# H and V of each octet in one block of TensorE, over three two-bank PSUM tiles

## The chip, the core and the metric

The kernel runs on one core of a Trainium2 chip. A core has a matrix engine (TensorE, PE in the profile, with its weight loads shown apart as PEld), a vector engine (VectorE, DVE), a scalar engine (ScalarE, ACT), GpSimd (POOL) and SyncE (SP), which here only issues transfers. Each engine works through its own list of instructions in order. The engines share SBUF, the working memory of 128 partitions, and PSUM, the memory that matmuls write, of 8 banks of 512 fp32 values per partition. DMA transfers are issued by SP, ACT or POOL and run beside the engines; a name with a q behind it (ACTq, SPq) is an engine's issuing part. The metric is the device time of one execution in microseconds (us).

## What is computed

Three terms are summed for a sequence of 2048 rows of 448 channels. Both branches take the layer-normalised first input.

```python
def _A_ref(q, k, v, shift_k, ssm_k, ssm_D):
    k_shift = sum of 4 shifted copies of k times shift_k       # short causal convolution
    kv = k_shift * v
    y = long causal convolution of kv with ssm_k, per channel (FFT of length 4096)
    return q * (y + kv * ssm_D)

def _B_ref(x, w1, b1, w2):
    h = einsum("bsd,df->bsf", x, w1) + b1                       # 448 -> 1792
    return einsum("bsf,fd->bsd", mish(h), w2)                   # 1792 -> 448

xn = _layernorm(A_q)
return A_q + _A_ref(xn, A_k, A_v, A_shift_k, A_ssm_k, A_ssm_D) + _B_ref(xn, B_w1, B_b1, B_w2)
```

## The kernel before

**The dense branch** is most of TensorE's work. It runs over 8 chunks of 256 rows and 7 pairs of 128-wide slices of the hidden layer, 56 pairs in all, numbered i. For each pair, `g1_mm(i)` makes the first product (22 matmuls of 256 columns, split into high and low parts XH, XL, w1h, w1l) in one PSUM bank; `mish(i)` reads that bank on ACT (two ACTIVATE), casts the result to `ach` on ACT and takes the rest `acl` on DVE; `g2_mm(i)` makes the second product (12 matmuls of 448 columns) in PSUM tiles `pg2`, two pairs later.

**Slots.** The program is written out by hand. Slot 2i holds `g1_mm(i)`. Slot 2i+1 holds `mish(i)` and `g2_mm(i-2)`. `at(slot, ...)` puts other work ahead of the dense work of a slot, `after(slot, ...)` behind it. No scheduler moves anything: the order written is the order on each engine. Small DVE pieces wait in a list `drip` and are taken out one by one by calls of `dv()`.

**The long convolution** goes through DRAM in stages. In slots up to 61 the columns of `ssm_k` and of `kv` are transformed (`f1_mm`) and stored to DRAM as Dh and Dkv. Then come 8 octets, the stage that is changed. For octet o:

- SP loads `ah` from Dh and `av` from Dkv (896 KB each) and the small factors `g` and `gi`.
- `h2_mm` makes H from `ah` in two PSUM tiles `pc` of two banks (real and imaginary part): 16 matmuls on 64x32 pieces of the array. `h2_out` copies H to SBUF (`hs`) on ACT, two copies.
- `v2_mm` does the same with `av` one slot later, and `v2_out` copies V to `vs` on ACT.
- `prod` multiplies both on DVE: six instructions of 128x896 (four products, one difference, one sum), in two parts in the two slots behind.
- `i1_mm` transforms the result back (16 matmuls on 32x64 pieces) into two `pc` tiles. `i1_out` copies them to `qe` on ACT, and ACT issues two stores to DRAM, to E.

V of octet o stands in slot 65+3o, H in the slot before it (octet 0: slot 63), the back transform in slot 69+3o, the last in slot 90. H, V and the back transform each stand ahead of the dense work of their slots, so each is a block of small matmuls between two runs of full-size ones. The tiles `pc` are taken in turn from a pool of two, four banks; the first product has two banks and the second two.

**The last transform.** From slot 92 POOL loads `e` from E (`e_load`), DVE folds each (`fold`, two instructions of 128x896), and `i2_mm` makes the last transform for two chunks at a time in slots 98, 102, 106 and 110, each followed by the gate with q. In the same slots the last chunk is normalised on DVE: `idr`, a row of means and factors, is loaded by SP (`nt_row`, slot 92 for its second half), `nt_norm` (two instructions, slot 94) uses it, and `nt_split` makes XH and XL of it. SP issues `q_load` for two chunks in slot 92, ahead of that row. The SBUF space of the octets is used again from slot 92 by tiles that wait until the last user of the space that they lie on is done.

## Time and profile before

| | us |
|---|---|
| median of 3 runs | 364.59 (364.45 to 365.19) |
| the profiled execution | 364.74 |
| its span, first to last instruction | 363.0 |
| PE busy | 357.0 (98% of the span) |
| DVE busy | 268.0 (74%) |
| ACT busy | 166.6 (46%) |
| POOL busy | 71.4 (20%) |

The profiled execution took 0.15 us more than the median. Around the span lie 1.74 us. An engine's busy time counts its instructions on the data; waiting and issuing are not in it. In rows of the timeline the first number is the start from the span's begin, the second the length, and `[... <-X]` is idle time before and what ended it. A row that ends in x16 stands for 16 records; TensorE shows two records for each fp32 matmul, so 16 matmuls of a block read x32. The granted TensorE clock was 1.00 in nearly all of the span.

### The profile page before, as it was taken

Reading aid. Unit: us, or ns where it says so; the run is one execution under the profiler, and the core shown is the slowest. Engines: PE = TensorE matmul, PEld = TensorE weight load, DVE = VectorE, ACT = ScalarE, POOL = GpSimd, SP = SyncE. Lnnn points to the kernel's source line nnn. Section 1 sums busy time; section 2 is a strip of 40 time slices with the busy share of each in tenths; the row PEclk is TensorE's granted clock in tenths of the full one; section 3 lists DMA queues with packets and bytes.
Section 4 is the critical chain, followed back from the end, with each engine's and each line's share of the span. In section 5 each row is a group of like instructions: output and inputs, shape, how many; then the busy total and the mean of one; then the engine's idle time right before and its main releaser. Section 6 shows DMA issues by size and latency. Waiting matters only on the chain.

```text
span 363.0 us, 7466 instructions
## 1 busy us (share of the span) xinstructions
PE 357.0 (98%) x3108; PEld 290.0 (80%) x3108; DVE 268.0 (74%) x367; ACT 166.6 (46%) x279; POOL 71.4 (20%) x66
## 2 busy tenths in 40 slices
PE   8999999999999999999999999999999999999995
PEld 2988888888888988988977666666666889889885
DVE  5999658999998988797427755767665744997641
ACT  4966553343424323334254555647655534225450
POOL 2136003722037224513000020000010005112020
PEclk9999999999999999999999999999999999999999
DMA  7998969758686438615877798998897486969655
GB/s 247 363 369 307 414 248 275 182 175 270 156 260 199 105 101 255 152 60 144 226 245 231 252 257 210 289 258 218 284 283 172 93 251 216 404 246 279 105 71 132
DMA packets 32451, 81.69 MB, mean 225 GB/s; under 512 B 2977, under 2 KB 18978, under 8 KB 32418
## 3 DMA queue, kind: packets, MB, share of 16 engines
q1 hardware_dynamic: 21266, 47.16, 39.3%
q10 hardware_dynamic: 8240, 19.38, 21.8%
q0 software_dynamic: 2912, 14.69, 13.5%
q8 instruction: 24, 0.39, 0.5%
q14 instruction: 9, 0.07, 0.1%
HBM read 52.77 MB, written 28.45 MB: 224 GB/s over the span
## 4 chain that ended last, share of the span: by engine, by line
PE 49%; DMA 4%; DVE 2%; ACT 1%; ACTq 1%; issue 0%
PE pg L499 18%; PE pg L528 7%; PE pc L219 6%; PE pg L530 6%; PE pg L529 6%; PE pc L262 4%; PE pc L319 2%; DMA av<-Dkv 2%; DMA Dkv<-st 2%; ACTq L273 1%; DVE st L140 1%; DVE x L183 1%; ACT a L507 0%; DVE qt L535 0%; DVE x L186 0%
## 5 line engine op out<-in xcount | busy, mean ns | idle before, releaser
L507 ACT ACTIVATE a<-pg,b1t 128x256 f32<-128x256 f32 x112 | 47.2, 473 | 108.7 <-PE pg L499 95.4
L499 PE MATMUL pg<-XH,w1h 128*128 128x256 f32 x448 | 90.6, 285 | 0.2 <-DVE XL L462 0.2
L499 PEld LDWEIGHTS pg<-XH,w1h 128*128 128x128 f32 x448 | 69.6, 188 | 18.6 <-issue 16.5
L528 PE MATMUL pg<-w2h,ach 128*128 128x448 f32 x224 | 83.2, 371 | 0.0
L530 PE MATMUL pg<-w2h,acl 128*128 128x448 f32 x224 | 81.4, 363 | 0.0
L80 DVE TENSOR_TENSOR acl<-a,ach 128x512 fp32r<-128x512 f32 x56 | 39.1, 698 | 57.1 <-ACT ach L79 57.0
L529 PE MATMUL pg<-w2l,ach 128*128 128x448 f32 x224 | 81.2, 362 | 0.0
L499 PE MATMUL pg<-XL,w1h 128*128 128x256 f32 x448 | 71.3, 277 | 0.0
L499 PEld LDWEIGHTS pg<-XL,w1h 128*128 128x128 f32 x448 | 60.2, 188 | 0.0
L499 PE MATMUL pg<-XH,w1l 128*128 128x256 f32 x336 | 56.8, 278 | 0.0
L528 PEld LDWEIGHTS pg<-w2h,ach 128*128 128x128 f32 x224 | 42.0, 187 | 14.4 <-issue 11.5
L499 PEld LDWEIGHTS pg<-XH,w1l 128*128 128x128 f32 x336 | 46.8, 188 | 0.0
L530 PEld LDWEIGHTS pg<-w2h,acl 128*128 128x128 f32 x224 | 42.1, 188 | 2.6
L529 PEld LDWEIGHTS pg<-w2l,ach 128*128 128x128 f32 x224 | 42.1, 188 | 2.4
L140 DVE TENSOR_TENSOR st<-pc,st 128x896 f32<-128x896 f32 x32 | 34.8, 1089 | 4.5 <-ACT st L136 3.8
L79 ACT CAST ach<-a 128x512 fp32r<-128x512 f32 x56 | 34.7, 620 | 1.8
L166 POOL TENSOR_TENSOR x<-kr,skb 128x896 f32<-128x896 f32 x8 | 17.0, 2130 | 78.2 <-DVE x L165 56.8
L183 DVE TENSOR_TENSOR x<-x 128x896 f32<-128x896 f32 x24 | 26.4, 1098 | 2.8 <-POOL x L166 2.2
L403 POOL TENSOR_TENSOR mv<-ve,mhalf 128x2 f32<-128x2 f32 x3 | 3.8, 1251 | 98.1 <-DVE ve L400 98.1
L136 ACT COPY st<-pc 128x896 f32<-128x896 f32 x16 | 14.5, 907 | 14.2 <-PE pc L130 12.6
L407 POOL TENSOR_SCALAR xn<-qt,mv,rstd 128x448 f32<-128x448 f32 x8 | 20.5, 2566 | 0.4
L270 ACT COPY qe<-pc 128x896 f32<-128x896 f32 x16 | 13.8, 912 | 12.0 <-PE pc L262 12.0
(83 smaller groups left out, 384.4 us busy)
## 6 DMA issues: line engine op xcount, KB each, us to landing
Dkv<-st ACTq DMA_DIRECT2D x16, 448.0 KB, 6.3
ah<-Dh SPq DMA_DIRECT2D x8, 896.0 KB, 7.9
av<-Dkv SPq DMA_DIRECT2D x8, 896.0 KB, 6.9
E<-qe ACTq DMA_DIRECT2D x16, 448.0 KB, 5.8
e<-E POOLq DMA_DIRECT2D x8, 896.0 KB, 8.4
kr<-in_k_dram SPq DMA_DIRECT2D x10, 448.0 KB, 6.4
Dh<-st ACTq DMA_DIRECT2D x10, 448.0 KB, 5.9
x<-in_hT_dram SPq DMA_DIRECT2D x8, 448.0 KB, 6.5
```

The costliest lines, as they stand in the source:

```text
L79: nc.scalar.copy(h, raw)
L80: V.tensor_sub(l, raw, h)
L140: f(st[:, n], e, st[:, 1])
L166: nc.gpsimd.tensor_mul(o, KR[g - u // 2], skb[:, u:u + 1].to_broadcast([128, 2, D]))
L183: V.tensor_add(KV[g], KV[g], o)
L219: nc.tensor.matmul(p[32 * t:32 * t + 32, r, :D], g[rs, t, c], a[rs, t], start=True, stop=True, tile_position=(64 * r, 32 * t))
L407: eng.tensor_scalar(xn[:, jj, :D], Q[c][:, jj], mv[:, j, 0:1], rs(c)[:, jj:jj + 1], op0=ALU.subtract, op1=ALU.mult)
L499: nc.tensor.matmul(ps[n], l, r, start=all(m[0] != n for m in seq[:n_]), stop=all(m[0] != n for m in seq[n_ + 1:]))
L507: nc.scalar.activation(a[:, n], ps[n], AF.Mish, bias=b1t[:, 2 * p + n:2 * p + n + 1])
L528: nc.tensor.matmul(ps, ah[:, n, cs], w2h[:, f], start=f == 0, stop=False)
L529: nc.tensor.matmul(ps, ah[:, n, cs], w2l[:, f], start=False, stop=False)
L530: nc.tensor.matmul(ps, al[:, n, cs], w2h[:, f], start=False, stop=f == NF - 1)
```

## The change

H and V of an octet become one block: `hv_mm(o)` issues the 16 matmuls of H, then the 16 of V, in slot 66+3o. The octets' back transform comes later: that of octet o-1 stands two slots behind octet o's block (the last two in slots 88 and 89).

V is no longer copied to SBUF. The four products on DVE read V straight from its PSUM tiles, so each V tile stays taken until two products have read it. `prod` is one piece behind the block: four products, then what is held back of `mish` in odd slots (its cast and `acl`), then difference and sum. In an odd slot with a block, `mish` is issued ahead of it.

PSUM: the two tiles `pq` and `pr` (two banks each) are made once for the whole program. `regroup(True)` in slot 66 closes the first product's pool of two banks and makes a third two-bank tile `pp` of them; `regroup(False)` in slot 92 turns it back. In between the first product writes a bank of whichever tile the table `GB` names. Each block therefore goes round: in an even slot H takes pp and pq, V takes pr and then pp again; in an odd slot H takes pr and pq, V takes pp and then pr again. So the second half of V waits until ACT has copied the first half of H.

SBUF: `av` gets a second buffer and is loaded a slot earlier; `hs` loses its second buffer, `vs` goes, `ya` and `yc` get a second one. The result of the last octet is copied to a buffer named `hs` instead of `qe`.

The stores to E are issued by GpSimd (`nc.gpsimd.dma_start`) instead of ACT.

On TensorE, an octet with its block in an odd slot stood so before, H and V on either side of a first product (`pc` the PSUM tiles, `pg` those of the dense branch):

```order
L219 MATMUL pc<-ah,g 32x448 x16
L499 MATMUL pg_2750<-XH,w1h 128x256 x3
L499 MATMUL pg_2750<-XH,w1l 128x256 x3
L499 MATMUL pg_2750<-XH,w1h 128x256
L499 MATMUL pg_2750<-XL,w1h 128x256 x4
L499 MATMUL pg_2750<-XH,w1h 128x256 x3
L499 MATMUL pg_2750<-XH,w1l 128x256 x3
L499 MATMUL pg_2750<-XH,w1h 128x256
L499 MATMUL pg_2750<-XL,w1h 128x256 x4
L219 MATMUL pc<-av,g 32x448 x16
```

Now an octet in an odd slot reads on TensorE, between the first product (which stands in pp) and the second:

```order
L508 MATMUL pp<-XH,w1h 128x256
L508 MATMUL pp<-XL,w1h 128x256 x4
L231 MATMUL pr<-ah,g 32x448 x8
L231 MATMUL pq<-ah,g 32x448 x8
L231 MATMUL pp<-av,g 32x448 x8
L231 MATMUL pr<-av,g 32x448 x8
L540 MATMUL pg_2051<-w2h,ach 128x448
```

The two blocks of 16 became one of 32, in four quarters of 8, of which the fourth writes the tile of the first.

On ACT, before, in the same stage, with the copies of H (hs) and V (vs) and the stores:

```order
L270 COPY qe<-pc 128x896 x2
L273 DMA E<-qe 64x4x448 x2
L507 ACTIVATE a<-pg_2543,b1t 128x256 x2
L79 CAST ach<-a 128x512
L230 COPY hs<-pc 128x896 x2
L239 COPY vs<-pc 128x896 x2
```

Now on ACT, around a block in an odd slot:

```order
L278 COPY qe<-pr 128x896
L278 COPY qe<-pq 128x896
L516 ACTIVATE a<-pp,b1t 128x256 x2
L244 COPY hs<-pr 128x896
L244 COPY hs<-pq 128x896
L80 CAST ach<-a 128x512
```

The stores and the copies of V are gone, and the cast of `mish` went behind the copies of H.

On SP, at the end of the octets, with the counters that each transfer waits for (DMAHW: transfers issued by SP or ACT; DMASW: by POOL), before:

```order
L285 DMA i_3452<-in_c_i_dram 128x64 [waits DMAHW6_49,DMAHW5_49]
L310 DMA q_3458<-in_q_dram 128x896 [waits DMAHW4_49,DVE_49,DMAHW6_49,PE_49,Activation_49]
L310 DMA q_3460<-in_q_dram 128x896 [waits DMAHW7_49,DVE_49]
L433 DMA idr<-MR 128x256 [waits DMAHW0_49,DVE_49]
L538 DMA out_dram<-qt 128x448 [waits DMAHW1_49,DVE_49]
```

and now:

```order
L293 DMA i_3346<-in_c_i_dram 128x64 [waits DMAHW5_49]
L318 DMA q_3352<-in_q_dram 128x896 [waits DMAHW2_49,DMAHW6_49,DMASW7_49,DMAHW7_49,DMASW0_49,Activation_49]
L318 DMA q_3354<-in_q_dram 128x896
L441 DMA idr<-MR 128x256 [waits DMAHW3_49,DMAHW0_49,DVE_49]
L550 DMA out_dram<-qt 128x448 [waits DMAHW1_49,DVE_49]
```

The first load of q lies on the SBUF space of `hs`. DMASW7 and DMASW0 are the two stores of the last octet, which now leave from `hs`, so this load, and behind it in SP's order the row `idr`, waits for them.

The diff, without two places where only a name of a tile changes:

```diff
--- before.py
+++ after.py
@@ -26,8 +26,7 @@
 H_AT = {2: 6, 3: 9, 0: 12, 4: 16, 5: 20, 6: 26, 7: 32}
 KV_AT = (24, 29, 34, 39, 44, 50, 55, 59)
 POOL_H = {20: (0, 2)}
-H0_AT = 63
-OCT_AT = (65, 3)
+OCT_AT = (66, 3)
 I2_AT = {98: (6, 7), 102: (0, 1), 106: (2, 3), 110: (4, 5)}
 LATE = 2
 NT = 5
@@ -47,9 +46,11 @@
     cp = pool("consts")
     wp = pool("weights")
     mp = pool("mlp")
-    g1p = pool("ps_g1", 2, space=PSUM)
     g2p = pool("ps_g2", 2, space=PSUM)
-    pcp = pool("ps_c", 2, space=PSUM)
+    psp = pool("ps_c", space=PSUM)
+    duo = [None] + [psp.tile([128, 2, 512], F32, name=n) for n in ("pq", "pr")]
+    psg = [ExitStack()]
+    g1p = [pool("ps_g1", 2, psg[0], space=PSUM)]
     dp = pool("scratch", space=DRAM)
 
 
@@ -79,9 +80,20 @@
         nc.scalar.copy(h, raw)
         V.tensor_sub(l, raw, h)
 
-    def pc():
-        return pcp.tile([128, 2, 512], F32, name="pc")
-
+    def pc(n):
+        return duo[n]
+
+    def bank(n):
+        return duo[n // 2][:, n % 2]
+
+    def pg():
+        return g1p[0].tile([128, 512], F32, name="pg1")
+
+    def regroup(wide):
+        psg.pop().close()
+        psg.append(ExitStack())
+        g1p[0] = psg[0].enter_context(tc.tile_pool(name="ps_g1", bufs=1 if wide else 2, space=PSUM, reuse_waits="tile"))
+        duo[0] = g1p[0].tile([128, 2, 512], F32, name="pp") if wide else None
 
     drip = []
 
@@ -122,7 +134,7 @@
 
     def f1_mm(src, g, key):
         x = src.pop(g)
-        PS[key, g] = ps = [pc(), pc()]
+        PS[key, g] = ps = [pc(1), pc(2)]
         for b in range(2):
             for h in range(2):
                 for jj in range(2):
@@ -189,7 +201,7 @@
 
     ph2 = ExitStack()
     sp2 = []
-    GT, AH, AV, HS, PV, Y = {}, {}, {}, {}, {}, {}
+    GT, AH, AV, HS, Y = {}, {}, {}, {}, {}
 
     def t2(shape, name, bufs=1):
         if not sp2:
@@ -202,7 +214,7 @@
             g = t2([128, 4, 2, 32], "g", 2)
             nc.sync.dma_start(g, c_g[:, o])
             GT[o] = [g]
-        d[o] = t2([128, 4, D], name)
+        d[o] = t2([128, 4, D], name, 2 if d is AV else 1)
         nc.sync.dma_start(d[o], src[16 * o:16 * o + 16].rearrange("(t a) n d -> (a n) t d", t=4))
 
     def gi_load(o):
@@ -210,8 +222,8 @@
         nc.sync.dma_start(gi, c_gi[:, o])
         GT[o].append(gi)
 
-    def f2_mm(a, o, c):
-        p = pc()
+    def f2_mm(a, o, c, n):
+        p = pc(n)
         g = GT[o][0]
         for t in range(4):
             for r in range(2):
@@ -220,41 +232,37 @@
                                  tile_position=(64 * r, 32 * t))
         return p
 
-    def h2_mm(o):
-        PS["H", o] = [f2_mm(AH[o], o, c) for c in range(2)]
-        AH.pop(o)
-
-    def h2_out(o):
-        HS[o] = t2([128, 2, 2, D], "hs", 2)
+    def hv_mm(o, hb, vb):
+        PS["H", o] = [f2_mm(AH[o], o, c, hb[c]) for c in range(2)]
+        h_out(o)
+        PS["V", o] = [f2_mm(AV[o], o, c, vb[c]) for c in range(2)]
+        AH.pop(o), AV.pop(o)
+
+    def h_out(o):
+        HS[o] = t2([128, 2, 2, D], "hs")
         for c, p in enumerate(PS.pop(("H", o))):
             nc.scalar.copy(HS[o][:, c], p[:, :, :D])
 
-    def v2_mm(o):
-        PS["V", o] = [f2_mm(AV[o], o, c) for c in range(2)]
-        AV.pop(o)
-
-    def v2_out(o):
-        PV[o] = t2([128, 2, 2, D], "vs")
-        for c, p in enumerate(PS.pop(("V", o))):
-            nc.scalar.copy(PV[o][:, c], p[:, :, :D])
-
-    def prod(o, part):
-        vs, hs = PV[o], HS[o]
-        vr, vi, hr, hi = vs[:, 0], vs[:, 1], hs[:, 0], hs[:, 1]
-        if part == 0:
-            Y[o] = a, c, b, e = [t2([128, 2, D], n) for n in ("ya", "yc", "yb", "yd")]
-            ops = ((V.tensor_mul, a, vr, hr), (V.tensor_mul, b, vi, hi), (V.tensor_sub, a, a, b))
-        else:
-            a, c, b, e = Y[o]
-            ops = ((V.tensor_mul, c, vr, hi), (V.tensor_mul, e, vi, hr), (V.tensor_add, c, c, e))
-            del PV[o], HS[o]
-        for f, *x in ops:
-            f(*x)
-            dv()
-
-    def i1_mm(o):
+    def prod(o):
+        vr, vi = (p[:, :, :D] for p in PS.pop(("V", o)))
+        hs = HS.pop(o)
+        hr, hi = hs[:, 0], hs[:, 1]
+        a, c = Y[o] = [t2([128, 2, D], n, 2) for n in ("ya", "yc")]
+        b, e = [t2([128, 2, D], n) for n in ("yb", "yd")]
+        for x, *y in ((a, vr, hr), (c, vr, hi), (b, vi, hi), (e, vi, hr)):
+            V.tensor_mul(x, *y)
+        for fn in held:
+            fn()
+        held.clear()
+        dv(2)
+        V.tensor_sub(a, a, b)
+        dv()
+        V.tensor_add(c, c, e)
+        dv()
+
+    def i1_mm(o, ib):
         gi = GT[o][1]
-        ps = [pc(), pc()]
+        ps = [pc(n) for n in ib]
         for c in range(2):
             for t in range(4):
                 ts = slice(32 * t, 32 * t + 32)
@@ -265,12 +273,12 @@
         Y.pop(o)
 
     def i1_out(o):
-        qe = t2([128, 4, D], "qe")
+        qe = t2([128, 4, D], "qe") if o < NO - 1 else t2([128, 2, 2, D], "hs").rearrange("p a b d -> p (a b) d")
         for i, p in enumerate(PS.pop(("I", o))):
             nc.scalar.copy(qe[:, 2 * i:2 * i + 2], p[:, :, :D])
         for r in range(2):
             k = 8 * (o % 4) + 4 * r
-            nc.scalar.dma_start(E.rearrange("p (k h) d -> p k h d", h=2)[:, k:k + 4, o // 4], qe[64 * r:64 * r + 64])
+            nc.gpsimd.dma_start(E.rearrange("p (k h) d -> p k h d", h=2)[:, k:k + 4, o // 4], qe[64 * r:64 * r + 64])
 
 
     ph3 = ExitStack()
...
@@ -467,19 +475,20 @@
         if jj == 0:
             dv(len(drip))
             x_tiles(c)
-        p = g1p.tile([128, 2, CH], F32, name="pg1").rearrange("p a b -> p (a b)")
+        p = pg()
         transposes(c, jj, p)
         for lo in range(2):
             x_split(c, jj, p, lo)
 
 
-    AHL, P1, P2 = {}, {}, {}
+    AHL, P1, P2, GB = {}, {}, {}, {}
+    held, hv = [], set()
     pairs = [(c, p) for c in range(NCHUNK) for p in range(NP)]
 
     def g1_mm(i):
         c, p = pairs[i]
         XH, XL = XS[c]
-        pt = [g1p.tile([128, 2, CH], F32, name="pg1") for _ in range(2 if i == 0 else 1)]
+        pt = [(bank(GB[i]) if i in GB else pg()).rearrange("p (a b) -> p a b", a=2) for _ in range(2 if i == 0 else 1)]
         ps = [pt[n % len(pt)][:, n] for n in range(2)]
         mm = [[], []]
         for n in range(2):
@@ -511,9 +520,12 @@
             w1_lo(2)
         ah = mp.tile([128, 2, CH], F32R, name="ach", bufs=3)
         al = mp.tile([128, 2, CH], F32R, name="acl", bufs=3)
-        split(ah, al, a)
-        dv()
         AHL[i] = ah, al
+        if 2 * i + 1 in hv:
+            held.append(lambda: split(ah, al, a))
+        else:
+            split(ah, al, a)
+            dv()
 
     def g2_mm(i, jjs=(0, 1)):
         c, p = pairs[i]
@@ -562,7 +574,8 @@
                 c, p = pairs[i]
                 if p == NP - 2 and c + 1 < NT:
                     ln_T(c + 1, 0)
-                mish(i)
+                if s not in hv:
+                    mish(i)
             if 0 <= j < n - 1:
                 g2_mm(j)
             elif j == n - 1:
@@ -608,20 +621,30 @@
         p and at(2 * p + (1 if p < 5 else 0), w2_load, p)
         at(2, w2_split, p) if p == 0 else after(2 * (p + G2_LAG) - 1, w2_split, p)
 
+    at(OCT_AT[0], regroup, True)
     for o in range(NO):
         s, d = OCT_AT[0] + OCT_AT[1] * o, OCT_AT[1]
-        h = s - 1 if o else H0_AT
-        (at if o else after)(h - d if o else h - 4, o_load, AH, Dh, o, "ah")
-        at(s - d if o else s - 2, o_load, AV, Dkv, o, "av")
-        at(h, h2_mm, o)
-        after(h, h2_out, o)
-        at(s, v2_mm, o)
-        after(s, v2_out, o)
+        hb, vb, ib = ((0, 1), (2, 0), (2, 1)) if s % 2 == 0 else ((2, 1), (0, 2), (0, 2))
+        (at if o else after)(s - d if o else s - 7, o_load, AH, Dh, o, "ah")
+        at(s - d - 1 if o else s - 3, o_load, AV, Dkv, o, "av")
+        at(s, hv_mm, o, hb, vb)
         at(s, gi_load, o)
-        after(s + 1, prod, o, 0)
-        after(s + 2, prod, o, 1)
-        at(s + 4, i1_mm, o)
-        after(s + 4, i1_out, o)
+        after(s, prod, o)
+        if s % 2:
+            hv.add(s)
+        if o == NO - 1:
+            ib = 0, 1
+        if o:
+            at(s + (2 if o < NO - 1 else 1), i1_mm, o - 1, ib)
+            after(s + (2 if o < NO - 1 else 1), i1_out, o - 1)
+        if s % 2 == 0:
+            GB[s // 2], GB[s // 2 + 1] = 2, 0
+        else:
+            GB[s // 2 + 1] = 2 if o < NO - 1 else 4
+    at(s + 2, i1_mm, o, ib)
+    after(s + 2, i1_out, o)
+    GB[s // 2 + 2] = 5
+    at(s + 5, regroup, False)
 
     ts = sorted(I2_AT)
     for n, t in enumerate(ts):
...
@@ -712,17 +735,20 @@
         j = s // 2 - G2_LAG - 1
         if s % 2 == 0 and j >= 0 and pairs[j][1] == NP - 1:
             g2_evac(pairs[j][0])
+        if s in hv:
+            mish(s // 2)
         for fn, args in plan.pop(s, ()):
             fn(*args)
         mlp_slot(s)
         fns = plan2.pop(s, ())
         for fn, args in fns:
-            if fn in (h2_out, v2_out, i1_out):
+            if fn is i1_out:
                 fn(*args)
         for fn, args in fns:
-            if fn not in (h2_out, v2_out, i1_out):
+            if fn is not i1_out:
                 fn(*args)
     assert not plan and not plan2
+    psg.pop().close()
     ph3.close()
 
 
```

More of the change, by code (lines that the diff above doesn't have):

```diff
@@ L312, in i2_mm @@
     def i2_mm(c):
-        p = pc()
+        p = pc(1 + c % 2)
         e = EE.pop(c)
@@ L682, in tile_kernel @@
     x_tiles(0)
-    fill = g1p.tile([128, 2, CH], F32, name="pg1").rearrange("p a b -> p (a b)")
+    fill = pg()
     def filler(n, w=wz):
```

## The prediction

> **What bounds the kernel now.** I read the page first, then the waits of TensorE, then stretches of the octet stage.
>
> ```profile
> span 363.0 us, 7466 instructions
> ...
> PE 357.0 (98%) x3108; PEld 290.0 (80%) x3108; DVE 268.0 (74%) x367; ACT 166.6 (46%) x279; POOL 71.4 (20%) x66
> ```
>
> TensorE works 357.0 of 363.0 us, so only what TensorE itself executes, or newly waits for, moves the end. Its waits after the start-up are two, both in the octet stage, 0.5 us together:
>
> ```profile
> PE pc L219 <- DMA av<-Dkv: 0.3, 1, 0.3
> ...
> PE pc L219 <- ACT hs L230: 0.2, 1, 0.2
> ```
>
> The stretches below are slots of that stage: H and a second product, V and a first product, the back transform and a second product; then, from ahead of the stage, a first and a second product without any block. The number behind the stretch is its length.
>
> ```profile
> 194.83:199.10 4.27, 4.27 (x45) 2.66 (x44) 3.06 (x4) 3.08 (x5) 0.00 (x0) 1.00 0.61 188
> 199.10:203.48 4.38, 4.38 (x56) 3.08 (x55) 3.46 (x6) 2.23 (x3) 0.00 (x0) 1.00 0.78 250
> 203.48:207.78 4.30, 4.30 (x46) 2.76 (x45) 2.88 (x6) 3.18 (x5) 0.00 (x0) 1.00 0.81 304
> 162.21:164.73 2.52, 2.52 (x24) 2.52 (x22) 2.52 (x6) 0.00 (x0) 1.69 (x1) 1.00 0.00 0
> 164.73:167.13 2.40, 2.40 (x15) 2.25 (x13) 2.37 (x5) 1.46 (x3) 1.56 (x1) 1.00 0.03 6
> ```
>
> A block of H costs 4.27 - 2.40 = 1.87 us, of V 4.38 - 2.52 = 1.86, a back transform 4.30 - 2.40 = 1.90. The inside of such a block:
>
> ```profile
> 194.83 1.73 PE L219 MATMUL pc<-ah,g 64*32 64x448 f32 x32
> ...
> 195.60 0.96 PE L219 MATMUL pc<-ah,g 64*32 64x448 f32 x16
> 195.98 0.58 PE L219 MATMUL pc<-ah,g 64*32 64x448 f32 x8
> 196.49 0.47 PE L528 MATMUL pg<-w2h,ach 128*128 128x448 f32 x1
> ```
>
> The rows are from narrow stretches of the timeline, so their starts show the groups of 8 records. Groups follow each other at 195.98 - 195.60 = 0.38 us. Four groups would be 1.52; the other 0.35 of the 1.87 us is paid per block, on the way in and out.
>
> **The change, part by part.** *One block instead of two* (TensorE). The 32 matmuls are the same, and so are their weight loads. Merged they are 8 groups: 8 x 0.38 + 0.35 = 3.39 us against 1.87 + 1.86 = 3.73. That saves 0.34 to 0.35 an octet, 8 x 0.35 = 2.8 us. The trace has no block of 8 groups. If nothing of the 0.35 were saved it would be 0; by the first group's own pitch (195.60 - 194.83 over two groups, 0.385) it is 8 x (3.73 - 8 x 0.385 - 0.33) = 2.6. I take 2.8, since the groups inside one block run at 0.38 already.
>
> *The two waits.* `av` of octet 0 landed at 188.03, when TensorE had stood for 0.3 us. Now its block begins in slot 66: H began at 180.79, and three slots without blocks (2.40 + 2.52 + 2.40) put it at 188.1, and V behind four groups at 189.6. The wait goes. The other was ACT being late with `hs`, because its stores to E held it. H of octet 0, and such a pair of stores:
>
> ```profile
> 180.79 0.98 PE L219 MATMUL pc<-ah,g 64*32 64x448 f32 x16
> ...
> 219.99 2.98 ACTq L273 DMA_DIRECT2D E<-qe  x2
> ```
>
> ACT no longer issues them, so this goes too: 0.5 us saved.
>
> *The ring of three tiles* (a new wait inside the block). The fourth quarter of the 32 matmuls needs the tile that ACT copies first.
>
> ```profile
> 207.78 1.74 PE L219 MATMUL pc<-ah,g 64*32 64x448 f32 x32
> ...
> 208.87 1.72 ACT L230 COPY hs<-pc 128x896 f32<-128x896 f32 x2 [1.87 <-PE pc L219]
> ...
> 212.16 1.36 PE L219 MATMUL pc<-av,g 64*32 64x448 f32 x24
> 212.27 0.84 ACT L507 ACTIVATE a<-pg,b1t 128x256 f32<-128x256 f32 x2 [1.68 <-PE pg L499]
> ```
>
> With ACT free, the first copy starts 1.09 us after the block and takes 1.72 / 2 = 0.86 to 0.91, so the tile is free at 2.00. The fourth quarter starts at 6 x 0.38 = 2.28. It fits with 0.28 to spare. In odd slots `mish` stands ahead on ACT: it starts 0.11 after the first product and takes 0.84, done at 0.95, ahead of 1.09. The next first product needs the second copy, done at 1.09 + 1.72 = 2.81, and starts at 196.49 - 194.83 + 4 x 0.38 = 3.18. Price 0; the upper end is a late ACT in all 8 octets.
>
> *V read from PSUM* (DVE, and tiles held longer).
>
> ```profile
> L80 DVE TENSOR_TENSOR acl<-a,ach 128x512 fp32r<-128x512 f32 x13 | 9.0, 692 | 25.7 <-ACT ach L79 25.7
> ...
> L252 DVE TENSOR_TENSOR ya<-vs,hs 128x896 f32<-128x896 f32 x8 | 8.7, 1087 | 7.7 <-PE pc L262 7.7
> ...
> L140 DVE TENSOR_TENSOR st<-pc,st 128x896 f32<-128x896 f32 x32 | 34.8, 1089 | 4.5 <-ACT st L136 3.8
> ```
>
> The groups are `acl`, a product from SBUF, and a sum of the same form with one side in PSUM: 1089 against 1087 ns, so the change of side costs nothing. V's first tile is written by 4 x 0.38 + 1.09 = 2.6 after the block's start, and four products end at 2.6 + 4 x 1.09 = 7.0. The tiles are wanted back two slots behind the block, at 3.39 + 2.40 + 2.52 = 8.3: covered by 1.3 us. [...] The 16 copies of V that go lay on ACT, beside TensorE; they free nothing at the end.
>
> *The loads.* `ah` keeps one buffer and is issued, as before, when H is done. Its landing (least, median, longest), and the median of `av`:
>
> ```profile
> DMA to landing us min/median/max: 4.9/7.9/8.0
> ```
> ```profile
> av<-Dkv SPq DMA_DIRECT2D x8, 896.0 KB, 6.9
> ```
>
> The 7.9 us fit into an octet's 12.7 us (three slots, 1.5 x (2.52 + 2.40), with blocks of 3.39 and 1.90) behind H's 1.66; `av` only starts earlier. Price 0, except in octet 1 (below).
>
> *The first odd block* (slot 69). ACT must first cast the second half of a normalised chunk (XH, slot 68), which waits for two `nt_norm` on DVE, and these now stand behind six instructions of `prod`.
>
> ```profile
> 200.19 1.42 DVE L439 TENSOR_TENSOR xn<-xn,idr 128x512 f32<-128x512 f32 x2
> ...
> 201.79 0.63 ACT L446 CAST XH<-xn 128x512 fp32r<-128x512 f32 x1
> ```
>
> Block 66 starts at 188.1; its products run from 190.7, with difference and sum six of 1.09, to 197.3; `acl` 0.69, norms 1.42, cast 0.63, `mish` 0.84: 200.8. The block of slot 69 starts at 188.1 + 3.39 + 2.52 + 2.40 + 2.52 = 198.9, and its V, four groups on at 200.4, needs the tile that this `mish` reads. V waits 0.4, and the fourth quarter 0.1 more for H's copy behind it. I take 0.5. The lower end is 0, as before the change; the upper 0.9: were `ah` of octet 1 to move only when `av` of octet 1 had landed, 188.0 + 6.9 + 4.9 = 199.8, the block itself would start 0.9 late, in the same place.
>
> *Stores to E by POOL.* POOL has time (20% busy). What matters is the last octet, where the row `idr` for the last normalisation now waits behind q for these stores to land:
>
> ```profile
> 290.99 0.63 PE L262 MATMUL pc<-ya,gi 32*64 32x448 f32 x8
> 292.78 1.72 ACT L270 COPY qe<-pc 128x896 f32<-128x896 f32 x2 [2.60 <-PE pc L262]
> ...
> 294.53 1.25 ACTq L273 DMA_DIRECT2D E<-qe  x2
> 299.46 0.33 SPq L433 DMA_DIRECT2D idr<-MR  x1
> 302.33 2.90 POOL L295 DMA_DIRECT2D e<-E  x4 [33.33 <-DMA idr<-MR]
> 302.54 1.41 DVE L439 TENSOR_TENSOR xn<-xn,idr 128x512 f32<-128x512 f32 x2
> 306.83 0.69 DVE L80 TENSOR_TENSOR acl<-a,ach 128x512 fp32r<-128x512 f32 x1 [2.89 <-ACT ach L79]
> 307.67 1.09 DVE L301 TENSOR_TENSOR ex<-e 128x896 f32<-128x896 f32 x1
> 311.53 1.09 DVE L303 TENSOR_TENSOR e<-e 128x896 f32<-128x896 f32 x1
> 313.29 0.54 PE L319 MATMUL pc<-ex,i 64*32 64x448 f32 x2
> ```
>
> The times to landing of 448 KB stores by ACT and by POOL, and of that row:
>
> ```profile
> E<-qe ACTq DMA_DIRECT2D x16, 448.0 KB, 5.8
> ...
> Dh<-st POOLq DMA_DIRECT2D x6, 448.0 KB, 8.6
> ...
> out_dram<-q POOLq DMA_DIRECT2D x5, 448.0 KB, 5.2
> ...
> idr<-MR SPq DMA_DIRECT2D x6, 128.0 KB, 5.6
> ```
>
> Up to here TensorE is 2.8 + 0.5 - 0.5 = 2.8 us ahead, and the last back transform stands ahead of a second product instead of behind it: it starts at 290.99 - 2.8 - 2.40 = 285.8. Its copies end 292.78 + 1.72 - 290.99 = 3.51 later, 289.3; POOL issues two stores at 2.90 / 4 = 0.73 each, the second at 290.0. It lands after 5.2 to 8.6; I take 6.5, the store's own 5.8 and 0.7 for the other path, since the 8.6 are stores of the kernel's start, where every queue was loading. So 296.5; two loads of q ahead, issued at 0.33 like the row, 297.2; the row's 5.6, 302.8; norms 1.41; `acl` 0.69: 304.9; then what took 307.67 to 311.53 + 1.09 = 312.62 before, the two folds with XL between, 4.95: 309.9. The second half of the last transform wants them at 313.29 - 2.8 = 310.5. It is covered by 0.6 us. At 5.2 it is covered by 1.9, at 8.6 TensorE waits 1.5. [...]
>
> **The sum.** 364.74 - 2.8 - 0.5 + 0.5 = 361.9 for the profiled execution; it stood 0.15 above the median, so against the median 361.8.
>
> **The rivals.** *The last stores land late* (slower). If POOL's second store takes longer than 7.1 us, `idr`, the norms and the folds, all in order on DVE, hold the last transform, us for us. The median of 8.6 costs 1.5 and gives 363.3. From 9.9 us on the whole gain is lost; at 10.8 it is 361.8 + 3.7 = 365.5. For it speaks the POOL row of 8.6, against it the later one of 5.2. Past the kernel before: 8%; landing between 7.1 and 9.9: 17%, 361.8 to 364.6.
>
> *The ring stalls.* 0.28 us of cover is little: were ACT's first copy 0.5 us late in every octet, TensorE would lose 8 x 0.2 = 1.8 and the time would be 363.5. Against it: 1.09 and 0.91 are measured with ACT free, and ACT has less to do than before. 9%.
>
> *Nothing saved per block.* If the 0.35 us belong to a change of operand or to the three new waits inside the block and not to leaving and entering the block shape, 2.8 falls away: 364.6, the same. The 0.38 us between groups inside one block, across a change of tile and weights, speaks against it. 6%.
>
> **How the numbers follow.** The forecast, no stall but the 0.5, with 0 to 0.9 in its place: 361.2 to 362.6, chance 60%. The measurement tells 0.2%, 0.73 us. Faster, below 363.86: 60 + 15 of the 17 + 7 of the 9 = 82; same: 6 + 2 + 2 = 10; slower: 8. For a wait that I have not seen I move 6 to slower, 3 from each: 0.79, 0.07, 0.14. The range 361.0 to 364.2 takes in 7.1 to 9.5 us of landing and the ring.
>
> **What would show it.** The waits of TensorE: none on `av`, about 0.5 us near 200 on ACT, none in the ring. H and V as one run of 64 records, 1.73 + 1.52 = 3.25 us long, and a slot with it and a second product 5.8 us. The second half of the last transform's first slot near 310.5; if it waits for DVE, the row `idr` will have been issued after 297.5. I am wrong if the slot with the merged block is over 6.0 us, or if `idr` goes out after 299.5.

## The result, and the profile after

The changed kernel takes 363.39 us (median of 13 runs, 362.47 to 364.37) against 364.44 for the kernel before it in the same comparison (364.18 to 365.19): a ratio of 0.997, with an interval of 0.9959 to 0.998. It is faster by 1.05 us, where 2.8 were forecast (361.8, in a range up to 364.2).

The head of the page after, and the waits of TensorE (the last number is the longest):

```profile
span 361.6 us, 7454 instructions
...
PE 355.9 (98%) x3108; PEld 291.0 (80%) x3108; DVE 265.7 (73%) x367; ACT 153.2 (42%) x263; POOL 80.9 (22%) x82
```
```profile
PE pg L683 <- DVE wz L679: 1.0, 1, 1.0
PE pr L327 <- DVE ex L309: 0.6, 1, 0.6
PE pg L508 <- DVE XL L470: 0.2, 1, 0.2
PE pr L327 <- DVE e L311: 0.2, 1, 0.2
```

The waits on `av` and on `hs` are gone, and there is none in the octet stage. New are two waits for the folds `ex` and `e` in the last transform (line 327), 0.8 us together.

The profiled span is 1.4 us shorter. Where that comes from is read from two stretches between the same TensorE instructions: from the first product of slot 62 to that of slot 92, which holds the whole octet stage, and from the last transform's first matmul to the first product behind it. Before, and then after:

```profile
178.18:297.69 119.51, 119.01 (x1279) 84.10 (x1278) 72.29 (x90) 64.32 (x97) 3.69 (x4) 1.00 0.82 234
```
```profile
178.05:293.77 115.72, 115.72 (x1280) 84.82 (x1278) 70.83 (x91) 50.93 (x81) 13.30 (x20) 1.00 0.80 238
```
```profile
312.51:314.18 1.67, 1.67 (x34) 0.49 (x33) 1.29 (x3) 0.00 (x0) 0.32 (x1) 1.00 1.03 412
```
```profile
308.58:312.85 4.27, 3.46 (x34) 0.63 (x33) 4.24 (x6) 0.00 (x0) 0.71 (x1) 1.00 1.02 408
```

The octet stage became 119.51 - 115.72 = 3.79 us shorter, and TensorE is busy in all of it. The first slot of the last transform became 4.27 - 1.67 = 2.60 us longer, with DVE at work for 4.24 of the 4.27. With 0.13 gained ahead of slot 62, 0.13 + 3.79 - 2.60 = 1.32, the span's 1.4 to a rounding. So the octets gave more than forecast, and two thirds of it was lost in one place, 15 us after the stage.

The slots in the octet stage (block and first product, block and second product, back transform and second product), after:

```profile
187.97:193.74 5.77, 5.77 (x88) 3.71 (x87) 3.63 (x5) 1.71 (x2) 0.00 (x0) 1.00 0.86 254
198.74:204.42 5.68, 5.68 (x77) 3.43 (x77) 4.25 (x6) 3.43 (x6) 0.00 (x0) 1.00 0.49 153
207.02:211.32 4.30, 4.30 (x46) 2.77 (x45) 2.40 (x5) 3.18 (x5) 2.02 (x3) 1.00 0.57 179
```

The first is in an even slot, so its product is a first one: 5.77 - 2.52 = 3.25 for the block; the second 5.68 - 2.40 = 3.28. The way into the block also lengthens the slot ahead (2.60 us from 196.14 to 198.74 for a first product that takes 2.52 alone), so that the whole block costs about 3.36. The back transform is what it was, 4.30.

Where the 2.60 were lost shows in the chain of waits (start, length, what), which in the kernel before did not run over this place:

```profile
296.20 8.79 DMA idr<-MR
305.01 0.70 DVE xn L447
306.35 0.68 DVE acl L81
307.03 1.01 DVE ex L309
308.20 0.87 issue
309.08 0.69 DVE XL L455
309.76 1.01 DVE ex L309
310.80 1.10 DVE e L311
311.94 0.97 PE pr L327 x12
```

The row `idr` for the last half of the last normalisation took 8.79 us to land; before, it was issued at 299.46 and its user on DVE ran at 302.54. Behind it stand, in order on DVE, the norms, `acl`, and the folds with `XL` between, to 311.89; TensorE had reached the transform at 308.58. The issues of this place, on SP and on POOL, after:

```profile
295.19 0.91 SPq L318 DMA_DIRECT2D q<-in_q_dram  x2
296.20 0.37 SPq L441 DMA_DIRECT2D idr<-MR  x1
```
```profile
288.47 1.25 POOL L281 DMA_DIRECT2D E<-hs  x2 [3.16 <-ACT hs L278]
295.67 2.89 POOL L303 DMA_DIRECT2D e<-E  x4 [5.95 <-DMA E<-hs]
```

Both queues wait for the last stores to E and are released together: the first load of `e` goes out 0.53 us ahead of the row. Before, the row was 2.9 us ahead of the loads of `e` (299.46 against 302.33).

Where the 8.79 us went is in the records of the DMA packets. SP's queue is q1, POOL's is q0; the numbers are packets, MB and share of the 16 DMA engines. From the row's issue to its first packet (296.20 to 299.66), and from there to the end of its last (304.35):

```profile
q1 hardware_dynamic: 283, 0.90, 78.1%
q0 software_dynamic: 34, 0.24, 17.2%
```
```profile
q0 software_dynamic: 196, 1.29, 78.0%
q1 hardware_dynamic: 143, 0.13, 15.1%
```

For the first 3.46 us SP's queue moved the two loads of q that stand ahead of the row. The first packet of `e` had started at 298.86, and the row's 128 packets of 1 KB then took 4.69 us among those of `e`. The landing was reported 0.64 us behind the last one. In the kernel before the three parts were 0.97, 1.71 and 0.28 us, with no packet of q or `e` beside the row.

### The profile page after: what moved, and what is told of

Read it like the earlier page. It is cut to its first block, busy times and chain, and to the rows that moved or that the text cites. A ratio compares the mean times of both kernels' runs of the same rounds, so it can differ in the third digit from the quotient of the medians.

```text
span 361.6 us, 7454 instructions
## 1 busy us (share of the span) xinstructions
PE 355.9 (98%) x3108; PEld 291.0 (80%) x3108; DVE 265.7 (73%) x367; ACT 153.2 (42%) x263; POOL 80.9 (22%) x82
## 4 chain that ended last, share of the span: by engine, by line
PE 50%; DVE 4%; DMA 2%; issue 1%; ACT 1%; DVEq 0%
PE pg L508 9%; PE pg L540 6%; PE pg L542 6%; PE pg L541 6%; PE pq L508 5%; PE pp L508 3%; PE pr L231 3%; PE pp L231 3%; DMA idr<-MR 2%; PE pp L270 2%; PE pq L231 2%; PE pr L508 1%; PE pr L270 1%; PE pr L327 1%; PE pq L327 1%
## 5 line engine op out<-in xcount | busy, mean ns | idle before, releaser
L516 ACT ACTIVATE a<-pg,b1t 128x256 f32<-128x256 f32 x86 | 36.3, 473 | 85.3 <-PE pg L508 75.0
L508 PE MATMUL pg<-XH,w1h 128*128 128x256 f32 x344 | 68.9, 283 | 0.2 <-DVE XL L470 0.2
L508 PEld LDWEIGHTS pg<-XH,w1h 128*128 128x128 f32 x344 | 53.8, 188 | 10.4 <-issue 8.6
L508 PE MATMUL pg<-XL,w1h 128*128 128x256 f32 x344 | 55.2, 277 | 0.0
L508 PEld LDWEIGHTS pg<-XL,w1h 128*128 128x128 f32 x344 | 46.4, 188 | 0.0
L508 PE MATMUL pg<-XH,w1l 128*128 128x256 f32 x258 | 43.7, 278 | 0.0
L152 DVE TENSOR_TENSOR st<-pq,st 128x896 f32<-128x896 f32 x32 | 34.8, 1089 | 4.3 <-ACT st L148 3.5
L508 PEld LDWEIGHTS pg<-XH,w1l 128*128 128x128 f32 x258 | 35.9, 188 | 0.1
L281 POOL DMA_DIRECT2D E<-qe x14 | 8.8, 630 | 63.7 <-ACT qe L278 63.6
L148 ACT COPY st<-pr 128x896 f32<-128x896 f32 x16 | 14.5, 908 | 13.9 <-PE pr L142 12.6
```

Of the source, the lines that this page charges most:

```text
L152: f(st[:, n], e, st[:, 1])
L508: nc.tensor.matmul(ps[n], l, r, start=all(m[0] != n for m in seq[:n_]), stop=all(m[0] != n for m in seq[n_ + 1:]))
L516: nc.scalar.activation(a[:, n], ps[n], AF.Mish, bias=b1t[:, 2 * p + n:2 * p + n + 1])
```

## The experiments

Three accounts of the lost 2.60 us were set against each other. Theory A: the row is slow because the loads of `e`, four of 896 KB, begin to move beside it. Theory B: it is only late, from its place on SP's queue behind a wait. Theory C: it is the stores of POOL, the rival that the prediction had priced. A fourth account, that the row stands behind the two loads of q on its own queue, was not set against them; the packets in the table below bear on it.

**The row ahead of the q loads** (row_first).

```diff
-        at(ts[0] - (6 if c < 2 else 4), q_load, c, nc.sync if c < 2 else nc.gpsimd)
+        at(ts[0] - 4, q_load, c, nc.sync if c < 2 else nc.gpsimd)
```

> The changed kernel with the two loads of q moved behind the row idr(7,1) on SP's queue, so that the row no longer stands behind a load that waits for the last stores to E; it now waits only for the first half's norms on DVE (which ended at 295.1 us in the changed kernel). Theory A, the row is slow because the loads of e begin to move beside it: it goes out at 295.2 instead of 296.2, about 0.5 us ahead of the first load of e instead of 0.5 behind, and lands in 3 to 6 us, at 298.5 to 301; the folds are then bound by e (landed 304.05 and 306.48 before) and the stall of the last transform falls from 2.6 to under 0.8: 361.0 to 361.8. Theory B, what costs is only the row's place behind the wait of the q loads: it lands 1.0 us earlier, and the time falls by 1.0, to 362.4.

361.29 us (361.16 to 361.36), ratio to the kernel before 0.9912 (0.9899 to 0.9925). Issues on SP and on POOL:

```profile
295.46 0.32 SPq L441 DMA_DIRECT2D idr<-MR  x1
295.96 1.10 SPq L318 DMA_DIRECT2D q<-in_q_dram  x2
```
```profile
296.42 2.89 POOL L303 DMA_DIRECT2D e<-E  x4 [6.38 <-DMA E<-hs]
```

The row went out 0.7 us earlier and landed in 3.6 us instead of 8.8; the waits for the folds are gone. Theory B's gain of 1.0 is too small for the 2.1 us. But the loads of q, which stood ahead of the row, are behind it here, so this run alone does not tell the loads of `e` from those of q.

**The stores back to ACT** (act_store), the change without its last part.

```diff
-            nc.gpsimd.dma_start(E.rearrange("p (k h) d -> p k h d", h=2)[:, k:k + 4, o // 4], qe[64 * r:64 * r + 64])
+            nc.scalar.dma_start(E.rearrange("p (k h) d -> p k h d", h=2)[:, k:k + 4, o // 4], qe[64 * r:64 * r + 64])
```

> The changed kernel with the stores to E issued by ACT again; everything else is as changed. Theory A: the last stores land within 0.7 us of where they did (295.1), row and loads of e still start together, and the time stays within 0.7 us of the changed kernel, 362.7 to 364.0. Theory C, the move of the stores to POOL is what costs (the rival that I had priced): the stall of 2.6 us goes, 360.8. ACT may lose 0.2 us a place to the stores again in the octets, as in the kernel before.

361.62 us in the median, but from 360.84 to 363.89. That is neither number: the median misses A's range, the spread covers both. In the profiled run the row went out 0.2 us behind the first load of `e` (296.00 against 295.80) and landed in 6.1 us, soon enough for the folds. So this kernel stands at the edge of the same race, and alone it does not clear POOL's stores. The next one does.

**The stores on POOL alone, in the kernel before** (before_pool), the same edit the other way round.

> The kernel before with the stores to E issued by POOL, and nothing else. Its q loads do not wait for these stores, so the row idr(7,1) keeps its 3 us ahead of the loads of e, under theory A: 364.1 to 364.7, the 0.2 us wait for hs gone, and e up to 0.7 us later or earlier. Theory C, POOL's stores are what costs in the changed kernel: they land late here too and the kernel is 1 us or more slower, 365.5 or more.

364.35 us, ratio 0.9998 (0.9989 to 1.0007): nothing. In the changed kernel, too, the last two stores landed within what the prediction took (6.5); their landing times, least, median and longest:

```profile
DMA to landing us min/median/max: 5.2/5.6/6.1
```

Theory C, that these stores land late, falls. That their move shifts the race of the row by some tenths is not excluded: the median of act_store is 1.8 us below the changed kernel.

**The row made late in the kernel before** (before_late_row). Three loads of 512 B from E stand ahead of the row on SP's queue. They bring nothing that is used; they wait for the last store to E, as the q loads do in the changed kernel.

```diff
+        if (c, jj) == (NCHUNK - 1, 1):
+            for r in (ve1[0:64], ve1[64:128], one[0:64]):
+                nc.sync.dma_start(r, E[:, 61, 0:2])
         nc.sync.dma_start(idr, MR[c][jj].partition_broadcast(128))
```

> The kernel before, with three tiny loads from E (512 B each, into scratch) put ahead of the row idr(7,1) on SP's queue; they wait for the last store to E, which landed at 301.5, so that the row goes out at about 302.5, beside or just behind the first load of e (302.33), instead of 3 us ahead of it. Theory A: the row lands in 6 to 9 us, at 308.5 to 311.5, instead of 302.42; norms 1.41, acl 0.6 and the two folds with XL 4.95 then end at 315.5 to 318.5 instead of 312.62, and the kernel is 2 to 6 us slower: 366.5 to 370.5. Theory B, a later row costs only its lateness: it lands in 3 us at 305.5, the norms end at 307, as acl did in the kernel before, and the time moves by under 0.5 us.

369.67 us, ratio 1.0136 (1.0121 to 1.0152): 5.1 us slower. Issues on SP and on POOL, the tile `idr`, and its user on DVE:

```profile
302.79 0.53 SPq L436 DMA_DIRECT2D idr<-MR  x1
```
```profile
301.68 2.89 POOL L295 DMA_DIRECT2D e<-E  x4 [32.74 <-DMA E<-qe]
```
```profile
DMA to landing us min/median/max: 8.5/8.5/8.5
```
```profile
311.32 1.42 DVE L442 TENSOR_TENSOR xn<-xn,idr 128x512 f32<-128x512 f32 x2 [8.76 <-DMA idr<-MR]
```

The row goes out 3.3 us later and lands 8.9 us later, so it is not only late, as B has it. None of the other parts of the change is in this kernel, so it is not C either. No large load stands ahead of the row on its own queue, but the three small ones do: their 192 packets of 8 bytes moved among those of `e` until 307.2, and the row's first packet started at 306.84. Its own packets then took 3.8 us among those of `e`, against 1.7 without them. So the loads of `e` do slow the row, as A has it, and part of that reaches it through what stands ahead on its own queue.

**A hold on the loads of e** (pool_wait, then pool_wait2): a POOL copy of one element from the row, ahead of the first load of `e`.

```diff
     def e_load(c):
+        if c == 6:
+            nc.gpsimd.tensor_copy(ve1[:, 0:1], idr[:, 0:1])
```

> The changed kernel with one small POOL copy from the row idr ahead of the first load of e, so that the loads of e are issued only when the row idr(7,1) has landed (one POOL instruction of one element more). Theory A: the row, alone, lands in 3 to 4 us (2.95 in the kernel before) at 299 to 300, the loads go out at 300 instead of 295.7 and the first lands in 5 to 6 us at 305 to 306, the second at 306.5 to 308; the folds end at 309 to 310, and the stall falls from 2.6 to between 0 and 1.2: 361.0 to 362.2, although the loads start 4 us later. Theory B, the row's landing does not depend on the loads: it lands at 305 as before, the loads go out after it, and the kernel is 5 us slower, 368.

362.58 us (362.30 to 363.67). The copy held nothing back: in the program it stood ahead of the row's load, so it read the row before, and the loads of `e` went out at 295.36, ahead of the row (296.00), which landed in 8.1 us. It is a repeat of the changed kernel and tells nothing between the theories. With the first two loads of `e` one slot later in the program it holds them:

```diff
-            at(ts[n - 2] + 1 if n > 1 else ts[0] - 6 + n, e_load, c)
+            at(ts[n - 2] + 1 if n > 1 else ts[0] - 5, e_load, c)
```

> The changed kernel with one small POOL copy from the row idr(7,1) ahead of the loads of e, now behind the row in the program, so that the loads of e go out only when the row has landed (in pool_wait the copy stood ahead of the row and read the row before it, so the loads did not wait). Theory A: the row, beside the q loads alone, lands in 3 to 4 us at 299.3 to 300.3, the first load of e goes out at 299.6 to 300.6 and lands in 5.3 to 6.5, at 305 to 307, the second 1.5 to 2.3 us later; the folds end at 309.5 to 311, and the stall falls from 2.6 to between 0.2 and 1.7: 361.2 to 362.6, although the loads start 4 us later than in the changed kernel. Theory B: the row lands at 305 and the kernel is 5 us slower, 368.

361.85 us (361.68 to 362.01), as A had it: the loads of `e` start 4.5 us later than in the changed kernel (300.16), and the kernel is faster by 1.5. One thing moved along: with the loads of `e` later in the program, those of q went out at 287, and the row straight behind the first half's norms, at 295.31; it landed in 3.8 us. So here both the loads of `e` and those of q are out of the row's way.

The nine places of the row, by the issues on the timeline, the first packets, and the row's time to landing:

| kernel | row issued | first `e` issued | row's first packet | first packet of `e` | row to landing | us |
|---|---|---|---|---|---|---|
| before | 299.46 | 302.33 | 300.43 | 303.77 | 3.0 | 364.44 |
| before_pool | 298.45 | 301.95 | 300.10 | 303.39 | 4.1 | 364.35 |
| row_early (below) | 288.33 | 296.22 | 290.81 | 299.50 | 5.1 | 360.95 |
| pool_wait2 | 295.31 | 300.16 | 296.36 | 301.59 | 3.8 | 361.85 |
| row_first | 295.46 | 296.42 | 296.41 | 300.15 | 3.6 | 361.29 |
| act_store | 296.00 | 295.80 | 298.87 | 299.99 | 6.1 | 361.62 |
| pool_wait | 296.00 | 295.36 | 299.11 | 298.47 | 8.1 | 362.58 |
| changed kernel | 296.20 | 295.67 | 299.66 | 298.86 | 8.8 | 363.39 |
| before_late_row | 302.79 | 301.68 | 306.84 | 303.14 | 8.5 | 369.67 |

The row takes over 8 us in the three kernels in which its first packet starts behind the first of `e`, and 3.0 to 6.1 in the others. In the four kernels in which it is issued behind `e`, its first packet also starts late, 2.9 to 4.1 us after the issue instead of 1.0 to 2.5, since q (until 299.70 in the changed kernel) or the three small loads are still moving ahead of it on SP's queue. The changed kernel without them was not run; an estimate from the 1.0 us of the kernel before and of row_first puts its row's first packet at 297.2, 1.7 us ahead of `e`. So the long landing took both: the loads of q ahead of the row and those of `e` beside it. The 5.1 us of row_early passed beside the last stores to E, and its user on DVE came 5 us after it had landed.

**The row a slot earlier** (row_early). The first half's norms need only a row that had landed long before; one slot earlier they free `idr` for the second row.

```diff
+            early = c == NCHUNK - 1
-            at(b + NT_AT["row"][jj], nt_row, c, jj)
-            after(b + NT_AT["norm"][jj], nt_norm, c, jj)
+            at(b + NT_AT["row"][jj] - early * jj, nt_row, c, jj)
+            after(b + NT_AT["norm"][jj] - early * (1 - jj), nt_norm, c, jj)
```

> The changed kernel with the first half's norms of the last chunk one slot earlier on DVE (they need only a row that landed at 277.0) and the row idr(7,1) one slot earlier, ahead of the loads of i and q on SP. The row then goes out at about 288.6, lands before the loads of e start, and the second half's norms never wait. Theory A: e lands by itself at 303 to 304 and 305.5 to 306.5, the folds end by 308.7, and TensorE stalls 0 to 0.3 us at the last transform instead of 2.6: 360.8 to 361.2. If the loads of e are what is late (theory D: the folds wait for e and not for the norms), the stall stays above 1 us: 362 or more.

360.95 us (360.83 to 361.20), ratio 0.9903 (0.9891 to 0.9916): the fastest, and 2.4 us below the changed kernel. The first slot of the last transform has its old length, with the loads of `e` moving as hard as ever (DMA share 1.02):

```profile
308.57:310.24 1.67, 1.67 (x34) 0.49 (x33) 1.05 (x2) 0.00 (x0) 0.32 (x1) 1.00 1.02 408
```

Two more runs on this kernel price the octet stage without the loss behind it.

**The block split again** (split4). Three of the second product's matmuls stand between H and V in the four octets in odd slots; `g2_one` issues these three, and `g2_mm` of that pair leaves them out.

```diff
         h_out(o)
+        if o % 2:
+            j = (OCT_AT[0] + OCT_AT[1] * o) // 2 - G2_LAG
+            g2_one(j, 0, 0)
+            ahead.add(j)
         PS["V", o] = [f2_mm(AV[o], o, c, vb[c]) for c in range(2)]
```

> row_early, with three matmuls of the second product (of its first group, one twelfth to a quarter of the slot) moved between H and V in the four octets that stand in odd slots; the matmuls are the same in number. Theory of the block cost: entering and leaving the tiled shape costs 0.35 to 0.41 us a block, so each of the four merged blocks becomes two again and TensorE loses 4 x 0.35 to 4 x 0.41, 1.4 to 1.65 us: 362.3 to 362.6 against 360.95. Rival: the saving came from something else of the merge (fewer waits, tiles held otherwise), and the split costs 0 to 0.3 us: 361.0 to 361.2.

362.41 us (362.29 to 362.67), 1.46 more: 0.37 us for each of the four blocks. The same slot, in row_early and split:

```profile
223.97:229.66 5.69, 5.69 (x78) 3.46 (x78) 3.02 (x4) 3.07 (x5) 0.66 (x2) 1.00 0.89 186
```
```profile
224.36:230.41 6.05, 6.05 (x77) 3.26 (x77) 2.42 (x3) 3.07 (x5) 0.65 (x2) 1.00 0.94 192
```

The same matmuls, the same tiles and waits, 0.36 us more for one more way in and out of the tiled shape.

**A later copy of H** (ring_late), to measure the cover of the ring of three tiles.

```diff
+        nc.scalar.copy(HS[o][:, 0, 0], PS["H", o][0][:, 0, :D])
         for c, p in enumerate(PS.pop(("H", o))):
```

> row_early, with half of H's first tile copied twice by ACT (one copy of 128x448 more ahead of the two, in every octet), so that the tile that V's fourth quarter needs comes free some 0.4 to 0.5 us later. By the cover that the prediction gave (tile free at 2.00 to 2.05 us after the block's start, fourth quarter at 2.28) V waits 0.15 to 0.3 us in each octet, 8 x that is 1.2 to 2.4, and the next first product in even slots, which needs the second copy, 0 to 0.2 more in each of four: 362.1 to 364.0 against 360.95. If the cover is larger than read (the matmuls of V run later than modelled, or the wait is not on this copy), nothing moves: 360.8 to 361.2.

363.91 us (363.75 to 364.45), 2.96 more than row_early, or 0.37 an octet. The first and the fourth quarter of a block on TensorE:

```profile
212.06 0.98 PE L231 MATMUL pp<-ah,g 64*32 64x448 f32 x16
...
214.67 0.99 PE L231 MATMUL pp<-av,g 64*32 64x448 f32 x16
```

The fourth quarter starts 214.67 - 212.06 = 2.61 us after the block's start. In row_early the same block starts at 211.31 and its fourth quarter 2.28 behind:

```profile
211.31 0.98 PE L231 MATMUL pp<-ah,g 64*32 64x448 f32 x16
...
213.59 0.96 PE L231 MATMUL pp<-av,g 64*32 64x448 f32 x16
```

On ACT the extra copy, 0.53 us with 0.03 behind it, moves the first copy of H back by 0.56, and V waits 2.61 - 2.28 = 0.33 for it. So the cover was 0.56 - 0.33 = 0.23 us. The expectation's upper end was 364.0, but its delay of 0.4 to 0.5 was too short.

## Why the prediction was wrong, point by point

**The bound**, TensorE, was right: 355.9 of 361.6 us busy, and all of the octet stage.

**One block instead of two** was right, and its size nearly so: 8 x 0.35 = 2.8 forecast. The three slots of an octet took 4.27 + 4.38 + 4.30 = 12.95 before; the three from 198.74 to 211.32 take 12.58, and the difference, 0.37, is what split4 found for one block. Eight octets are 8 x 0.37 = 2.96. The merged block was forecast at 3.39 and costs 3.36.

**The two waits** went, as forecast, but they were worth more than the 0.5 read from the list of waits: 3.79 - 2.96 = 0.83 is left for them. By the starts of the kernel before, the first product ahead of the late V ran from 184.97 to 188.03, 3.06 us where the one ahead of H (178.18 to 180.79) took 2.61, and the second product held by `hs` took 2.88 instead of 2.61. That is 0.45 + 0.27 = 0.72; the last 0.1 stays open.

**The first odd block** was forecast to wait 0.5 us and did not wait. The steps were right and their sizes a bit too long. DVE after, around slot 68, and ACT:

```profile
190.63 1.09 DVE L253 TENSOR_TENSOR ya<-pr,hs 128x896 f32<-128x896 f32 x1 [2.14 <-PE pr L231]
...
195.63 1.08 DVE L260 TENSOR_TENSOR yc<-yc,yd 128x896 f32<-128x896 f32 x1
196.64 0.69 DVE L81 TENSOR_TENSOR acl<-a,ach 128x512 fp32r<-128x512 f32 x1
197.24 1.41 DVE L447 TENSOR_TENSOR xn<-xn,idr 128x512 f32<-128x512 f32 x2
```
```profile
198.69 0.62 ACT L454 CAST XH<-xn 128x512 fp32r<-128x512 f32 x1 [3.25 <-DVE xn L447]
199.21 0.83 ACT L516 ACTIVATE a<-pp,b1t 128x256 f32<-128x256 f32 x2
```

Six instructions of 1.09 us start 1.00 us apart, since each begins before the one ahead has ended. That makes 6.0 us where the prediction added 6.5. The two ACT instructions overlap by 0.1 as well. `mish` ended at 200.04 instead of 200.8, and V, at 200.27, was not held. Times of rows were added where starts would have had to be.

**The ring** was right: no wait in it, and the cover of 0.28 is 0.23 by ring_late. The rival's price, 8 x 0.2 for a copy 0.5 us late in every octet, is 8 x 0.27 by the measured cover (and its own sum, 361.8 + 1.8, is 363.6 and not 363.5). In ring_late an octet lost 0.37, of which V's wait is 0.33; where the other 0.04 went stays open.

**V read from PSUM** cost nothing: the products take 1081 to 1092 ns, where 1087 were read from SBUF.

```profile
L253 DVE TENSOR_TENSOR ya<-pr,hs 128x896 f32<-128x896 f32 x4 | 4.4, 1092 | 13.1 <-PE pr L231 13.1
L253 DVE TENSOR_TENSOR yb<-pr,hs 128x896 f32<-128x896 f32 x4 | 4.3, 1081 | 0.0
```

**Stores to E by POOL**: this is the step that failed, in one of its terms. The second store was taken to go out at 290.0 and to land in 6.5 us; it went out at 289.1 and landed in 6.1. The 0.7 that the 6.5 holds for the other path is shown by no run: the 14 stores to E by POOL before these two landed in 6.0 us in the median, where ACT's 16 had taken 5.8. The term behind it, "the row's 5.6", was 8.8. The prediction took the median of all six rows, and for the two loads of q ahead it added only the time to issue them, 0.7 us. The row had to stand behind their data, 3.46 us from its issue to its first packet, and then move among the packets of `e`, 4.69 us. The prediction had the loads of `e` in its own fence, 3 us behind the row, and did not see that the change sets them beside it, since both now wait for the same two stores. The folds then took 4.94 us, as forecast (4.95). And TensorE was further ahead than the sum had it (3.92 instead of 2.8), so it wanted them at 309.4 instead of 310.5. Had the row landed in 5.6, from 296.20, it would have been there at 301.8. In act_store it landed at 302.05, the first fold waited 0.26 us for `e`, and TensorE waited for no fold. So the 2.60 would have gone, and the time would have been 363.39 - 2.60 = 360.8, an estimate.

**The rivals.** None of the three came. The nearest in place was the first (the last stores late): the same chain, the same stall, another link. The sign that the prediction gave for it, the row issued after 297.5, was the wrong one: the row was issued at 296.20, early, and still held everything. It was written for a row that is late, not for one that is slow. That the measured 363.39 lies next to this rival's 363.3, and inside the range, is luck.

**The sum**, with the measured sizes: 364.74 - 0.13 - 3.79 + 2.60 = 363.4, the measured median.

## What to carry to other kernels

Where a change makes two queues wait for the same event, look at what they issue behind it: a small load that the critical chain needs should not start together with a set of large ones that it does not need yet, nor stand behind other loads on its own queue: here the row took 8.1 to 8.8 us where it did both, and 3.0 to 5.1 clear of those loads. Give the small one its own earlier slot, which cost nothing here (360.95 us, the fastest of all), rather than a place in a race of half a microsecond. And a gain on TensorE moves the time at which every later hand-over is due, here by 3.92 us; each cover behind it has to be worked out against the new due time.

## What the runs showed of the hardware that was not expected

**The row of 128 KB took as long as the loads of 896 KB beside it.** Where its first packet started behind the first of `e`, in the changed kernel and in before_late_row, the row landed between the first and the last of the four loads. Their landing times, after:

```profile
DMA to landing us min/median/max: 8.4/10.9/13.2
```

The first landed at 295.67 + 8.4 = 304.1, the row at 305.0, the last at 297.8 + 13.2 = 311.0. In before_late_row the first landed in 5.9 us, at 307.6, the row at 311.3. From 299.66 to 304.35 the row's 128 packets are spread among those of `e` in the changed kernel. Most of `e`'s take 0.27 us and most of the row's 0.05; many records of both lasted longer, up to 0.9 and 0.4 us. In this stretch `e`'s queue filled 78.0% of the 16 engines' time and the row's queue 15.1%. How an engine chooses between two queues no run shows. The report came 0.64 us behind the row's last packet, against 0.28 in the kernel before; what the difference is was not shown either.

**The race shows as scatter.** The changed kernel, act_store and pool_wait, in which the row and `e` start within 1.2 us of each other by their first packets, vary by 1.9, 3.1 and 1.4 us. Row_first, row_early and pool_wait2, where the row is clear of `e`, and before_late_row, where it is far behind, vary by 0.2 to 0.4. This is a hint and no more: the last four were run 4 or 5 times each, and the kernel before and before_pool, with the row clear, vary by 1.0 and 1.5 us over 13 and 11 runs.

**The list of TensorE's waits shows a part of a stall.** It gives 0.8 us for the last transform, where the slot lost 2.60; the weight loads (PEld) list 1.4, 1.0 and 0.5 us there. For ring_late it gives 0.2 us in the ring:

```profile
PE pp L231 <- ACT hs L245: 0.2, 1, 0.2
```

The kernel lost 2.96 us there. The ends of matmuls are modelled in this profile, and TensorE is listed as busy for 3.46 of the 4.27 us of the slot that is 1.67 long without a stall, so most of the stall counts as busy. The two old waits of the octet stage, 0.5 us in the list, were 0.72 by the starts. The length of a slot between two instructions that stand in both kernels showed every loss.
